# Gate and up tiles of two blocks at once, in seven products over gate/up, feature halves and blocks

## The chip, the cores and the metric

The kernel runs on one core of a Trainium2 chip. The metric is the device time of one execution in microseconds; the median of three runs is given. Five engines work side by side, each in the order of its own queue: TensorE (PE in the profile, its weight loads are PEld), VectorE (DVE), ScalarE (ACT), GpSimd (POOL) and SyncE (SP), which here issues every DMA.

## The reference, cut to what matters

A transformer block in fp32 on 2048 tokens with D = 576 features: attention with 32 query heads and one shared key and value head, then a bilinear feed-forward part with F = 4608 hidden features, both behind a layer norm and with a residual.

```python
h  = x + attention(layernorm(x)) @ wo
g  = layernorm(h) @ w_gate            # (2048, 576) @ (576, 4608)
u  = layernorm(h) @ w_up              # the same shape
h2 = h + (g * u) @ w_down             # (2048, 4608) @ (4608, 576)
```

## The kernel before, in words

Every fp32 product is made of three passes on rounded parts (type fp32r): each operand is split into a high part (a cast) and a low part (the operand minus its high part), and high x high, high x low and low x high are added in PSUM. `split` does it: the cast on the engine in `self.cast` (in the feed-forward part ScalarE, `act.copy`) or on one that is passed in, the subtraction on VectorE.

The tokens go in four blocks of 512 (`TB`), the hidden features in 36 tiles of 128 (`NF`), two tiles making a pair. `keys_values` and the loop behind it in `run` make keys, values and all queries, with the first block's attention between them: one round of that loop makes two attention steps (`pair`) and takes as much from `queries` as `RATE` allows. Then `blocks` runs `ffn(b)` for b = 0 to 3. The order of all engines' instructions is the order in which this Python code issues them (a manual schedule); there is no planner.

- `ffn(b)` makes, for each tile, `gate` and `up` by 27 matmuls each (9 groups of 64 features x 3 passes) on 64 rows of the array: gate on rows 0 to 63, up on rows 64 to 127, so that the two of a pair run side by side. `split_w` takes the weights (`wr`) apart, the cast on GpSimd, one tile ahead; `load_w` loads the next. Then `g` is copied from PSUM by ScalarE, and VectorE multiplies it with `up` into `hf`.
- The attention of blocks 1 to 3 runs between these matmuls while there is some left (`on`), two blocks ahead; it ends in tile 5 of block 2. From there to the end the tiles are made without it, with gate and up in one two-bank PSUM tile `gu`, of which there are two.
- `left_first`, `left` and `left_sums` prepare a pair of `hf` tiles for the down projection, which uses seven products instead of eight on a 2 x 2 split (a Strassen-Winograd scheme): four sums `S`, and the splits into `self.A`.
- `down(b, pair)` makes the down projection of a pair: 14 stages (`STAGES`) of three matmuls with full 128 rows and 288 columns, in three PSUM banks; 8 of the stages are added to the residual `h` by VectorE, 6 are copied to `tmp` by ScalarE and added by GpSimd. The weights `wdo` (seven tiles of 288 KB a pair) were split in block 0, stored to `wd_dram`, and are loaded by `load_wd` into ten buffers. The last pair of a block has 48 matmuls and no sums.
- `spread(b + 1)` transposes the next block's normed tokens into `X` and copies each half of the rows to the other by DMA, so that both row halves have them.
- `aux` is a queue of small things (normalising heads, output projections `project`, layer norm statistics and `scales`), taken in `run_aux` once or twice a tile.

Of the kernel before, what the change touches and what calls it, by code (L numbers as in the profile page):

```python
# [54 lines left out]
class Block:  # L55


    def __init__(self, tc, x, wq, wkv, wo, wo0, wgu, wd, cst, out):
# [3 lines left out]
        self.wgu, self.wd, self.cst, self.out = wgu, wd, cst, out  # L62
        self.pe, self.act, self.dve, self.sp = tc.nc.tensor, tc.nc.scalar, tc.nc.vector, tc.nc.sync
# [678 lines left out]
    def project(self, b, c):  # L742
# [27 lines left out]
        if c == 4:  # L770
            if b == 0:
                self.statistics(b, NQ - 1)
                self.normed[b] = self.mv, self.rstd(self.mv[:, :, 1], f"b{b}")
            else:
                last = b == NB - 1
                for i in range(4):
                    self.aux.append((self.round + i // 2, lambda i=i: self.some_statistics(b, i), self.within if last else None))
                if last:
                    self.aux.append((self.round + 2, lambda: self.scales(b), self.within))

# [6 lines left out]
    def some_statistics(self, b, s):  # L787

        self.statistics(b, s)
        if s == NQ - 1 and b < NB - 1:  # L790
            self.scales(b)
# [63 lines left out]
    def load_w(self, n):  # L855

        if n < NF * NB:
            r = self.wr[n] = self.wp.tile([P, 9, P], F32, tag="wr", bufs=1, name=f"wr{n}")
            self.sp.dma_start(r, self.wgu[n % NF])

    def split_w(self, n):
        if n < NF * NB:
# [37 lines left out]

    def down(self, b, pair):

        pe, dve, act, sp, pool = self.pe, self.dve, self.act, self.sp, self.nc.gpsimd
        h = self.h[b]
        W = [self.wdo.pop((b, pair, j), None) for j in range(7)]
        if pair == NC - 1:
            ys = {}

            def part(s, n, i):

                ms = [(self.A[:, k, 2 * i + s // 2], W[(1, 0, 2, 3)[2 * i + n]][:, l]) for k, l in ((0, 0), (0, 1), (1, 0))]
                for j, (m, k) in enumerate(ms):
                    pe.matmul(ys[s, n][:, :HD], m[:, s % 2 * P:(s % 2 + 1) * P], k, start=(i == j == 0), stop=(i == 1 and j == 2))  # L913
# [37 lines left out]
        for i, (t, bank, (x, w), first, (s, n), on_dve) in enumerate(STAGES):  # L951
            y = banks[bank]
            ms = [(self.A[:, k, x], W[w][:, l]) for k, l in ((0, 0), (0, 1), (1, 0))]
            for j, (m, k) in enumerate(ms):
                pe.matmul(y[:, :HD], m[:, t * P:(t + 1) * P], k, start=(first and j == 0), stop=(j == 2), skip_group_check=True)  # L955
            hs = h[:, t + 2 * s, n * HD:(n + 1) * HD]
            if on_dve:
                dve.tensor_tensor(hs, hs, y[:, :HD], ALU.add)  # L958
# [16 lines left out]
    def ffn(self, b):  # L975
        pe, act, dve = self.pe, self.act, self.dve
        X, hid, todo = self.X, [], None
        for f in range(NF):
            n_ = NF * b + f
# [10 lines left out]
            for c in range(9):  # L990
                for wk, xk in ((0, 0), (0, 1), (1, 0)):
# [52 lines left out]
            if f < NF - 1 and (on or not todo):  # L1044
                self.run_aux()
            todo = (f // 2,) if k else None
        if b + 1 < NB:
            both(self.spread(b + 1), self.down(b, *todo))
# [3 lines left out]
        else:  # L1052
            drain(self.down(b, *todo))

# [44 lines left out]
    def right(self, p):  # L1099
# [20 lines left out]
        self.load_raw(p + 1)  # L1120

    def begin(self, first):

        self.first = first
        self.wd_list = [(b, p, j) for b in range(first, NB) for p in range(NC) for j in (range(4) if p == NC - 1 else ORDER)]
        self.n_wd = 0
# [4 lines left out]
    def blocks(self):  # L1131
# [34 lines left out]
        self.load_x(2)  # L1166
        for b in range(NB):
            self.ffn(b)
        del self.A, self.o_hl, self.S, self.tmp, self.X, self.ob, self.mv

    def run(self):
# [3 lines left out]
        self.wd_dram = tc.dram_tile([NC, P, 7, 2, HD], F32, name="wd_dram")  # L1175
        self.m_dram = tc.dram_tile([NB, 2, H, TB], F32, name="m_dram")
        self.known, self.n_mx = [0] * NB, 0
        self.tqs, self.acc_at = [], 0
        self.begin(True)
        with ExitStack() as st:  # L1180
# [11 lines left out]
            with tc.tile_pool(name="p0q", bufs=1) as self.p0q:  # L1192
# [4 lines left out]
                with tc.tile_pool(name="qb", bufs=2) as self.qb:  # L1197
# [5 lines left out]
                    self.cast = self.dve.tensor_copy  # L1203
                    live, due = True, 0.0
                    while live:
                        if self.n_pair >= WO_FROM and not self.wo_r0:
                            for c in range(EARLY):
                                self.load_wo_0(c)
# [7 lines left out]
                        self.run_aux(1)  # L1216
                        self.flush(len(self.pend) - 1)
            self.wp, self.hh, self.late, self.hp2 = pool("w", 2), pool("hid", 4), pool("P3", LATE), pool("resid2", 1)
            self.blocks()
# [43 lines left out]
def f32(ap):  # L1263
    return ap.bitcast(F32)
# [100 lines left out]
```

## Time and profile before

| | |
|---|---|
| median of three runs | 2322.93 us (2322.11 to 2326.28) |
| the profiled execution | 2324.7 us, span of its instructions 2322.9 us |
| TensorE busy | 2285.7 us, 98% of the span |
| VectorE, ScalarE, GpSimd busy | 1202.2, 1410.1 and 684.9 us |
| first layer, keys and queries | to about 270 us |
| last attention step | 1674 us |
| block 2's tile 12 to the end | 1742 to 2322.9 us |

Busy times are unions over instructions; a matmul's end is modelled, so that neighbours overlap, and the time of one is read from the distance of starts. "Idle before, releaser" says how long an engine stood still before an instruction and which instruction's end let it go.

### The profile page before, as it was taken

To read this page: it belongs to the slowest core of one execution; us is meant where nothing else is said; L and a number is where in the kernel's file an instruction comes from. 1 tells how busy PE (TensorE), PEld (TensorE's weight loads), DVE (VectorE), ACT (ScalarE), POOL (GpSimd) and SP (SyncE) were. 2 spreads that over 40 slices of the span, in tenths; PEclk is the share of its full clock that TensorE was granted. 3 is DMA by queue.
4 is the path that set the end of the run, shared out by engine and by line. 5 is a ranking of instruction groups with operands and counts; after the bars stand their busy time and mean duration, and the time that the engine had idled before them with its cause. 6 is when DMAs were issued, how large, how long until landed. Compare 5 with 4: busy or idle time off the path is not lost.

```text
span 2322.9 us, 45901 instructions
## 1 busy us (share of the span) xinstructions
PE 2285.7 (98%) x18114; PEld 1589.5 (68%) x18114; DVE 1202.2 (52%) x2152; ACT 1410.1 (61%) x1877; POOL 684.9 (29%) x856
## 2 busy tenths in 40 slices
PE   7999999999999999999999999999999999999998
PEld 5333345676667666667766667766788888888887
DVE  8333435565565575434434444434476666466665
ACT  5899887767676767676776677676623233232322
POOL 4000003444354345212212212212233333333332
PEclk9999999999999999999999999999999999999999
DMA  5222305433442433543424333324354445554553
GB/s 172 80 77 70 99 30 154 148 108 122 141 149 94 140 132 113 182 138 113 122 84 129 113 95 119 126 88 151 106 184 169 169 169 183 195 169 169 175 180 123
DMA packets 127130, 306.76 MB, mean 132 GB/s; under 512 B 17553, under 2 KB 17681, under 8 KB 126265
## 3 DMA queue, kind: packets, MB, share of 16 engines
q1 hardware_dynamic: 126905, 303.73, 39.7%
q8 instruction: 145, 2.38, 0.4%
q14 instruction: 80, 0.66, 0.1%
HBM read 233.76 MB, written 55.67 MB: 125 GB/s over the span
## 4 chain that ended last, share of the span: by engine, by line
PE 79%; ACT 7%; DVE 6%; issue 4%; DMA 3%; SPq 1%; POOL 0%; ACTq 0%; DVEq 0%; POOLq 0%
PE acc L601 19%; PE y L955 16%; PE gu L997 13%; PE pg L997 12%; PE s L596 11%; ACT P L597 5%; PE yo L759 3%; PE pu L997 3%; PE psq L448 2%; DVE ws L89 1%; ACT room L88 1%; DVE hf L1031 1%; DVE S L892 1%; PE y L913 1%; DMA ob<-ob 1%
## 5 line engine op out<-in xcount | busy, mean ns | idle before, releaser
L597 ACT ACTIVATE P<-s 128x1024 f32<-128x1024 f32 x1024 | 1000.9, 1030 | 340.9 <-PE s L596 248.3
L997 PE MATMUL pu<-X,ws 64*128 64x512 f32 x2106 | 571.6, 390 | 0.4 <-DVE hf L1031 0.4
L997 PE MATMUL pg<-X,ws 64*128 64x512 f32 x2106 | 570.4, 389 | 0.0
L601 PE MATMUL acc<-P,V 128*32 128x512 f32 x4096 | 483.8, 597 | 0.0
L596 PE MATMUL s<-q,kT 56*128 56x512 f32 x2048 | 428.3, 426 | 11.5 <-ACT P L597 9.5
L997 PEld LDWEIGHTS pg<-X,ws 64*128 64x128 f32 x2106 | 389.9, 185 | 69.0 <-issue 1.2
L955 PE MATMUL y<-wdo,room 128*128 128x288 f32 x2856 | 414.9, 301 | 4.9 <-DVE h L958 4.4
L997 PE MATMUL gu<-X,ws 64*128 64x512 f32 x3564 | 417.0, 390 | 1.8 <-POOL ws L88 1.0
L955 PEld LDWEIGHTS y<-wdo,room 128*128 128x128 f32 x2856 | 386.9, 188 | 41.1 <-issue 23.6
L997 PEld LDWEIGHTS pu<-X,ws 64*128 64x128 f32 x2106 | 389.1, 185 | 5.6 <-DVE hf L1031 0.8
L997 PEld LDWEIGHTS gu<-X,ws 64*128 64x128 f32 x3564 | 341.9, 185 | 68.7 <-issue 6.2
L596 PEld LDWEIGHTS s<-q,kT 56*128 56x128 f32 x2048 | 192.0, 184 | 229.6 <-ACT P L597 132.4
L963 POOL TENSOR_TENSOR x<-x,tmp 128x288 f32<-128x288 f32 x204 | 157.6, 806 | 495.1 <-ACT tmp L962 494.8
L962 ACT COPY tmp<-y 128x288 f32<-128x288 f32 x408 | 163.0, 401 | 225.6 <-PE y L955 201.9
L88 POOL CAST ws<-wr 128x1152 fp32r<-128x1152 f32 x144 | 170.9, 1187 | 376.7 <-DMA wr<-in_wgu_dram 211.0
L601 PEld LDWEIGHTS acc<-P,V 128*32 128x32 f32 x4096 | 111.1, 109 | 249.0 <-issue 245.9
L89 DVE TENSOR_TENSOR ws<-wr,ws 128x1152 fp32r<-128x1152 f32 x144 | 201.4, 1399 | 96.1 <-POOL ws L88 94.7
L963 POOL TENSOR_TENSOR h<-h,tmp 128x288 f32<-128x288 f32 x204 | 158.9, 809 | 237.2 <-ACT tmp L962 237.0
L958 DVE TENSOR_TENSOR x<-x,y 128x288 f32<-128x288 f32 x272 | 117.8, 454 | 205.4 <-PE y L955 205.4
L1031 DVE TENSOR_TENSOR hf<-pu,g 128x512 f32<-128x512 f32 x78 | 54.0, 692 | 273.6 <-ACT g L1027 273.6
L958 DVE TENSOR_TENSOR h<-h,y 128x288 f32<-128x288 f32 x272 | 117.2, 453 | 83.9 <-PE y L955 83.6
L1027 ACT COPY g<-gu 128x512 f32<-128x512 f32 x66 | 38.9, 589 | 161.7 <-PE gu L997 161.7
(172 smaller groups left out, 1713.9 us busy)
## 6 DMA issues: line engine op xcount, KB each, us to landing
wdo<-wd_dram SPq DMA_DIRECT2D x369, 288.0 KB
wr<-in_wgu_dram SPq DMA_DIRECT2D x144, 576.0 KB
wd_dram<-wdo SPq DMA_DIRECT2D x123, 288.0 KB
q<-q_dram SPq DMA_DIRECT2D x64, 216.0 KB
raw<-in_wd_dram SPq DMA_DIRECT2D x36, 288.0 KB
q_dram<-qs SPq DMA_DIRECT2D x15, 504.0 KB
X<-X SPq DMA_DIRECT2D x24, 256.0 KB
ob<-ob SPq DMA_DIRECT2D x121, 36.0 KB
```

The source lines that it names most:

```text
L88: (copy or self.cast)(hi, src)
L89: self.dve.tensor_tensor(lo, src, f32(hi), ALU.subtract)
L596: self.pe.matmul(s_[:, i], self.kT[o:o + 56, t * P:(t + 1) * P], q[o:o + 56, pr], start=True, stop=True)
L597: self.act.activation(p_, s_, AF.Exp, scale=SCALE)
L601: self.pe.matmul(acc[32 * j:32 * j + 32, :], self.V[:, t, :], Ps[j // 2][:, j % 2, :], start=(t == 0), stop=(t == NT - 1), skip_group_chec ...
L759: pe.matmul(y[:, :HD], m, k, start=(i == 0), stop=(i == len(ms) - 1))
L955: pe.matmul(y[:, :HD], m[:, t * P:(t + 1) * P], k, start=(first and j == 0), stop=(j == 2), skip_group_check=True)
L958: dve.tensor_tensor(hs, hs, y[:, :HD], ALU.add)
L962: act.copy(z, y[:, :HD])
L963: pool.tensor_tensor(hs, hs, z, ALU.add)
L997: pe.matmul(ps, w[o:o + 64, wk, c], X[o:o + 64, xk, c], start=(j == 0), stop=(j == 26))
L1031: dve.tensor_tensor(hf, pu, g, ALU.mult)
```

## The change

Blocks 0 and 1, and the first `F1 = 12` tiles of block 2, stay as they are. What was left of the feed-forward part is done by a new function, `two_blocks`:

- the first 12 tiles of block 3 alone, in four products a tile: gate and up, each over two halves of the features. A half is 288 features: two groups of 128 rows, each in three passes, and a tail of 32 features whose three passes lie in 96 rows of one matmul. So a product has seven matmuls, all with more than 64 rows.
- the other 24 tiles for blocks 2 and 3 together. The 2 x 2 split is now over gate/up, feature halves and blocks, and seven products (with sums of weights on one side and differences of tokens on the other) take the place of eight.

The sums of the weights are made once, by `sums`, in the rounds of the projection loop, on GpSimd and VectorE, one step in each round, and are kept in DRAM (`s_dram`, and `t_dram` for the split tails). In `two_blocks` each product's weights are loaded (`load_raw_operand`), cast by ScalarE and completed by VectorE (`ahead`), five (alone: four) products ahead, with tails eight (six) ahead. Block 3's tokens are transposed in `transposed`, called step by step from `prepare` in block 2's tiles; the differences of tokens are made by `differences`, one step after each product of block 3's own tiles. `down` takes its left operand as an argument, and in the joint stage blocks 2 and 3 use the same loaded `wdo`. In the diff's core, `tt` and `add` are VectorE's `tensor_tensor`.

```diff
@@ project
-                             lambda: b in self.h and (c in self.wos and not (self.odd and (b == NB - 1 or b == 1 and c < 3)) if b else c in self.wo_in)))
+                             lambda: b in self.h and (c in self.wos and not (self.odd and self.more(NB) and (b == NB - 1 or b == 1 and c < 3)) if b else c in self.wo_in)))
                 for i in range(4):
-                    self.aux.append((self.round + i // 2, lambda i=i: self.some_statistics(b, i), self.within if last else None))
+                    self.aux.append((self.round + i // 2, lambda i=i: self.some_statistics(b, i), None))
@@ down
+        A = A or (self.A[:, 0], self.A[:, 1])
+        both = b == 2 and pair >= F1 // 2
         W = [self.wdo.pop((b, pair, j), None) for j in range(7)]
+        if both:
+            self.wdo.update(((b + 1, pair, j), w) for j, w in enumerate(W))
@@ ffn
-        for f in range(NF):
+        for f in range(F1 if b == 2 else NF):
...
+                    if n_ == N_OLD - 1 and j in (5, 20):
+                        self.first_operands(j > 5)
...
-                self.run_aux()
+                self.run_aux(1 + (b == 2))
+                self.prepare()
...
-            drain(self.down(b, *todo))
+            self.two_blocks(todo[0])
+    def tail(self, t, r):
+        self.act.copy(t, r)
+        self.dve.tensor_tensor(t[32:64], r[32:64], f32(t[32:64]), ALU.subtract)
...
+    def load_raw_operand(self, n):
+        if n < len(SEQ):
+            f, o = SEQ[n]
+            src = self.wj[f, o] if o < 4 else self.s_dram[f - F1, :, o - 4]
+            self.sp.dma_start(self.raws[n % 8], src.rearrange("p (c m) -> p c m", c=2))
+
+    def ahead(self, tails, splits):
+        while self.n_tail < min(tails, len(SEQ)):
+            f, o = SEQ[self.n_tail]
+            self.sp.dma_start(f32(self.slot(self.n_tail)[0:96, 4]), self.t_dram[f // 9, :, f % 9, o])
+            self.n_tail += 1
+        while self.n_split < min(splits, len(SEQ)):
+            w = self.slot(self.n_split)
+            self.split(w[:, 0:2], w[:, 2:4], self.raws[self.n_split % 8])
+            self.load_raw_operand(self.n_split + 8)
+            self.n_split += 1
+
+    def product(self, bank, n, B, first):
+        w, (hi, lo, t) = self.slot(n), B
+        ms = [(w[:, i + 2 * k], (hi, lo)[l][:, i]) for i in range(2) for k, l in ((0, 0), (0, 1), (1, 0))] + [(w[0:96, 4], t)]
+        for j, (a, m) in enumerate(ms):
+            self.pe.matmul(bank, a, m, start=(first and j == 0), stop=(j == 6), skip_group_check=True)
+        joint = n >= 4 * F1
+        self.ahead(n + 1 + (8 if joint else 6), n + 1 + (5 if joint else 4))
+
+    def left_parts(self, last, hf, A):
...
+        self.split(A[0][:, 0], A[1][:, 0], a11)
+        dve.tensor_tensor(S[:, 0], a21, a22, ALU.add)
+        dve.tensor_tensor(S[:, 1], S[:, 0], a11, ALU.subtract)
+        yield
+        dve.tensor_tensor(S[:, 2], a11, a21, ALU.subtract)
+        dve.tensor_tensor(S[:, 3], a12, S[:, 1], ALU.subtract)
+        yield
+        self.split(A[0][:, 3:7], A[1][:, 3:7], S)
+        yield
+        self.split(A[0][:, 1:3], A[1][:, 1:3], two(hf[1]))
+        yield
+
+    def two_blocks(self, pair):
...
+        queue = [(2, pair, (x() for x in [self.left_sums]))]
+        work = self.differences()
...
+        for f in range(F1):
+            head = queue.pop(0) if queue else None
+            for i, (bank, B) in enumerate(((x, 0), (x, 1), (y, 0), (y, 1))):
+                self.product(bank, n, self.B[B], i % 2 == 0)
...
+                if head:
+                    next(head[2], None)
+                if i == 1:
+                    act.copy(g, x)
+                if f:
+                    next(work, None)
+            dve.tensor_tensor(hf, y, g, ALU.mult)
...
+            if f % 2:
+                queue.append((3, f // 2, self.left_parts(False, hid, A)))
+            finish(head)
...
+        for f in range(F1, NF):
+            head = queue.pop(0) if queue else None
+            plan = [(x, 0, True), (y, 1, True), (x, "T2", False), (z, "T3", True), (x, "T1", False), (z, "T4", False), (x, "B22", False)]
+            for i, (bank, B, first) in enumerate(plan):
+                self.product(bank, n, self.B[B], first)
+                n += 1
+                if i == 0:
+                    act.copy(p1, x)
+                elif i == 1:
+                    add(p1, p1, y)
+                elif i == 2:
+                    act.copy(u2, x)
+                elif i == 3:
+                    act.copy(p7, z)
+                elif i == 4:
+                    add(p7, p7, x)
+                elif i == 5:
+                    add(u2, u2, z)
+                    dve.tensor_tensor(h3, p1, u2, ALU.mult)
+                if head:
+                    next(head[2], None)
+            dve.tensor_tensor(h2, p7, x, ALU.mult)
...
+            finish(head[:3] if head else None)
...
+        for b, p, parts, to in queue:
+            drain(self.down(b, p, to))
@@ sums
+    def sums(self):
...
+        def four(a, s):
...
+        for f in range(F1, NF):
+            a, s = f32(v[:, f % 2, 0]), f32(v[:, f % 2, 1])
+            four([a[:, o] for o in range(4)], [s[:, o] for o in range(4)])
+            yield
+            sp.dma_start(self.s_dram[f - F1], s)
+            load(f + 2)
+            yield
+F1 = 12
+N_OLD = 2 * NF + F1
+SEQ = [(f, o) for f in range(F1) for o in range(4)] + [(f, o) for f in range(F1, NF) for o in (0, 1, 5, 6, 4, 3, 7)]
```

`differences` has 28 steps: twelve subtractions or additions and four casts of 1024 columns, then six DMAs, and tails of 96 rows. `transposed` has three: the normed tokens (ScalarE, with copies of the tails on GpSimd); 16 transposes and their splits; eight transposes of tails and their parts. `finish` drains a queued pair's parts, issues its `down` and then the next `wdo` loads; after each second joint tile the pair is queued for block 2 and for block 3, to be taken one in each of the next two tiles. `four` makes four sums or differences of 256 columns on GpSimd. `sums` has 89 steps; those ahead of the ones shown make the sums of the tails, split them, and store 14 MB in `t_dram`.

More of the change, by code (lines that the diff above doesn't have):

```diff
@@ L789, in some_statistics @@
         self.statistics(b, s)
-        if s == NQ - 1 and b < NB - 1:
+        if s == NQ - 1:
             self.scales(b)
@@ new lines, in slot, with first_operands @@
+    def slot(self, n):
+        first = 4 * F1
+        return self.slots[n % 6 if n < first else (n - first) % 8]
+    def first_operands(self, split):
+        if not split:
+            self.slots = []
+            self.more_slots()
+            self.raws = [r[:, i] for t in ("wr", "wos") for r in [self.wp.tile([P, 4, 2, P], F32, tag=t, bufs=1, name=f"{t}_j")] for i in range(4)]
+            self.n_tail = self.n_split = 0
+            for n in range(8):
+                self.load_raw_operand(n)
+            self.ahead(3, 0)
+        else:
+            self.ahead(3, 3)
@@ new lines, in more_slots @@
+    def more_slots(self):
+        w = self.wp.tile([P, 3, 5, P], F32R, tag="ws", bufs=2, name=f"ws_j{len(self.slots)}")
+        self.slots += [w[:, i] for i in range(3)]
+    def load_raw_operand(self, n):
[13 more added lines that the diff above has]
+            self.n_split += 1
@@ new lines, in product @@
+    def product(self, bank, n, B, first):
[6 more added lines that the diff above has]
+    def left_parts(self, last, hf, A):
+        dve, S = self.dve, self.S
+        two = lambda x: x.rearrange("p (a q) -> p a q", a=2)
+        if last:
+            for i in range(2):
+                self.split(A[0][:, 2 * i:2 * i + 2], A[1][:, 2 * i:2 * i + 2], two(hf[i]))
+                yield
+            return
+        (a11, a21), (a12, a22) = (halves(x, HT) for x in hf)
+        self.split(A[0][:, 0], A[1][:, 0], a11)
+        dve.tensor_tensor(S[:, 0], a21, a22, ALU.add)
+        dve.tensor_tensor(S[:, 1], S[:, 0], a11, ALU.subtract)
+        yield
+        dve.tensor_tensor(S[:, 2], a11, a21, ALU.subtract)
+        dve.tensor_tensor(S[:, 3], a12, S[:, 1], ALU.subtract)
+        yield
+        self.split(A[0][:, 3:7], A[1][:, 3:7], S)
+        yield
+        self.split(A[0][:, 1:3], A[1][:, 1:3], two(hf[1]))
+        yield
@@ L1166, in blocks @@
         self.load_x(2)
-        for b in range(NB):
+        for b in range(NB - 1):
             self.ffn(b)
         del self.A, self.o_hl, self.S, self.tmp, self.X, self.ob, self.mv
+        del self.B, self.slots, self.raw, self.raw_tails, self.spare, self.prep
     def run(self):
@@ L1204, in run @@
                     live, due = True, 0.0
+                    sums = self.sums()
                     while live:
+                        next(sums, None)
                         if self.n_pair >= WO_FROM and not self.wo_r0:
@@ L1217, in run @@
                         self.flush(len(self.pend) - 1)
+                    drain(sums)
             self.wp, self.hh, self.late, self.hp2 = pool("w", 2), pool("hid", 4), pool("P3", LATE), pool("resid2", 1)
```

194 lines of the change are left out of this document (180 added, 14 removed).

## The prediction

> **What bounds the kernel now.** I read the page first (busy times, the chain that ended last), then a table of stretches, then the timeline of one cycle late in block 3. In order: the page's busy line and chain; the stretches (columns: stretch, its length, busy us of PE, PEld, DVE, ACT and POOL with instruction counts, granted clock, DMA share, GB/s); pieces of the chain.
>
> ```profile
> PE 2285.7 (98%) x18114; PEld 1589.5 (68%) x18114; DVE 1202.2 (52%) x2152; ACT 1410.1 (61%) x1877; POOL 684.9 (29%) x856
> PE 79%; ACT 7%; DVE 6%; issue 4%; DMA 3%; SPq 1%; POOL 0%; ACTq 0%; DVEq 0%; POOLq 0%
> ...
> 15.50:20.00 4.50, 3.82 (x16) 2.63 (x17) 4.37 (x9) 1.54 (x4) 4.15 (x4) 1.00 0.84 350
> 66.00:270.00 204.00, 204.00 (x1495) 77.23 (x1495) 60.96 (x110) 184.33 (x191) 0.00 (x0) 1.00 0.22 70
> 1742.40:2322.90 580.50, 568.17 (x4576) 489.40 (x4572) 350.64 (x592) 171.88 (x336) 207.43 (x241) 0.99 0.50 170
> ...
> 2060.31 6.36 PE gu L997 x53
> 2302.92 6.37 PE gu L997 x54
> ```
>
> From 1742 us on (block 2's tile 12 to the end) attention is over, and 568 of 580 us are matmul: only fewer or denser matmuls help there. The two chain pieces stand 13 cycles apart; a cycle is two feature tiles and one `down`, (2302.92 - 2060.31)/13 = 18.66 us. VectorE is 60% busy there, so it has room, but not twice over.
>
> The last 33 matmuls of one `down`, and a whole later cycle, in the timeline (start, us, engine, line, operation, count), in pieces cut small where single matmuls matter, with the durations that I use below:
>
> ```profile
> 1955.19 4.70 PE L955 MATMUL y<-wdo,room 128*128 128x288 f32 x33 [0.16 <-DVE h L958]
> ...
> 2053.54 0.61 PE L997 MATMUL gu<-X,ws 64*128 64x512 f32 x4
> 2054.09 0.53 PE L955 MATMUL y<-wdo,room 128*128 128x288 f32 x2
> 2059.94 0.86 DVE L958 TENSOR_TENSOR h<-h,y 128x288 f32<-128x288 f32 x2 [0.36 <-PE y L955]
> 2059.74 0.57 PE L955 MATMUL y<-wdo,room 128*128 128x288 f32 x3
> 2060.24 0.50 PE L997 MATMUL gu<-X,ws 64*128 64x512 f32 x2
> ...
> 2060.24 12.54 PE L997 MATMUL gu<-X,ws 64*128 64x512 f32 x108
> 2061.44 0.41 ACT L88 CAST room<-hf 128x256 fp32r<-128x256 f32 x1 [0.95 <-DVE hf L1031]
> 2063.59 0.42 DVE L89 TENSOR_TENSOR room<-hf,room 128x256 fp32r<-128x256 f32 x1
> 2066.75 0.59 ACT L1027 COPY g<-gu 128x512 f32<-128x512 f32 x1 [4.90 <-PE gu L997]
> 2067.37 0.69 DVE L1031 TENSOR_TENSOR hf<-gu,g 128x512 f32<-128x512 f32 x1 [3.36 <-ACT g L1027]
> 2067.63 1.15 POOL L88 CAST ws<-wr 128x1152 fp32r<-128x1152 f32 x1 [5.35 <-DMA wr<-in_wgu_dram]
> 2068.09 0.62 ACT L88 CAST room<-hf 128x512 fp32r<-128x512 f32 x1 [0.76 <-DVE hf L1031]
> 2068.09 0.96 DVE L892 TENSOR_TENSOR S<-hf,hf 128x256 f32<-128x256 f32 x1
> 2069.43 0.42 DVE L894 TENSOR_TENSOR S<-hf 128x256 f32<-128x256 f32 x1
> 2070.10 0.69 DVE L89 TENSOR_TENSOR room<-hf,room 128x512 fp32r<-128x512 f32 x1
> 2070.22 1.05 ACT L88 CAST room<-S 128x1024 fp32r<-128x1024 f32 x1 [1.51 <-DVE S L895]
> 2071.30 1.23 DVE L89 TENSOR_TENSOR room<-S,room 128x1024 fp32r<-128x1024 f32 x1 [0.51 <-ACT room L88]
> ```
>
> 54 pairs in 12.54 us, the last taking 0.39: (12.54 - 0.39)/53 = 0.229 a pair, 0.232 with the first pair's delay spread in. A matmul of `down` is (4.70 - 0.30)/32 = 0.1375, so 42 are 5.8 us.
>
> **The change, part by part.**
>
> *Fewer matmuls.* Now a tile of one block is 27 pairs of 64-row matmuls (gate beside up). After it, a tile of block 3 alone is 4 products of 7 matmuls = 28, and a tile of both blocks together 7 x 7 = 49 instead of 54. Over the range: 24 x 54 + 12 x 27 = 1620 slots become 24 x 49 + 12 x 28 = 1512, 108 fewer. What does a 128-row, 512-column matmul take? The key and query projections at the start are such:
>
> ```profile
> 34.36 3.41 PE L236 MATMUL psk<-XT,wk 128*108 128x512 f32 x14
> 1710.49 0.58 PE L955 MATMUL y<-wdo,room 128*128 128x288 f32 x3
> 1710.90 0.30 PE L759 MATMUL yo<-wos,room 128*128 128x288 f32 x1
> 274.02 1.35 PE L479 MATMUL psg<-tq,G 126*32 126x512 f32 x5
> L479 PE MATMUL psg<-tq,G x21: 388/397/426, 26.1 to 275.0; 126*32 126x512 f32 x17, 72*32 72x512 f32 x4
> ```
>
> (3.41 - 0.39)/13 = 0.232, the same as a pair. So 108 x 0.232 = **-25.1 us**.
>
> *No change of row grouping.* Today every `down` (128 rows) stands between tiles of 64 rows. The last pair before it ends at 2053.54 + 0.61 = 2054.15, so it began at 2053.76, and the first matmul of `down` begins at 2054.09: 0.33 us later where 0.23 is usual, some 0.09 lost. The first two matmuls of `down` end 0.53 after their start, so the second began 0.23 after the first where 0.1375 is usual: another 0.10. Going back, the last matmul of `down` begins at 2059.74 + 0.57 - 0.30 = 2060.01 and the next pair at 2060.24, 0.09 late, and that pair takes 0.50 instead of 0.39. So about 0.19 us each way. From `down` to the output projection, 128 rows after 128, the step is 1710.90 - (1710.49 + 0.28) = 0.13: nothing lost. In the range there are some 60 such changes (29 of `L955` and one of `L913` both ways), and in the new code everything has full rows: 60 x 0.19 = **-11.4 us**. Against it: the seventh matmul of each product has 96 rows, and if that were a grouping of its own, 216 products with two changes each would cost 216 x 2 x 0.19 = +82 us. But of the five `psg` matmuls above four have 126 rows and one 72, and all go in 1.35 us, (1.35 - 0.40)/4 = 0.24 each. I take nothing for it. The Trainium skill ("TensorEngine Tiling (Array Packing)", Key Properties) says that changing the tiling mode drains TensorE; the trace agrees, with 0.19 us each. Its list of configurations has 128, 64 and 32 rows, so by it too the tail is no mode of its own; taken as a drain at every change of a tile's shape it would speak against this change, with those 82 us.
>
> *Joint tiles: what VectorE and ScalarE must do.* Casts of weights go from POOL (one of 1152 columns) to ScalarE, seven of 256 columns a tile (0.41 each), with seven VectorE subtractions (0.42); three PSUM copies on ScalarE (0.59); three adds and two products of 512 on VectorE (0.69). Each tile also has a full left preparation (four sums of 0.42, splits of 256, 1024 and 512) and a `down` (8 adds). VectorE: 7 x 0.42 + 5 x 0.69 + 4 x 0.42 + 0.42 + 1.23 + 0.69 + 8 x 0.45 = 14.0 us of a tile's 49 x 0.232 + 5.8 = 17.2 us: 82%, and 10.4 of the 11.4 us of the products alone. There is one bank each for x, y and z, and x is read and rewritten within the tile, so the order counts. I follow one tile (product i ends at 1.62 x (i+1); an eviction starts 0.24 after the product, as `g` at 2066.75 after 27 pairs from 2060.24; both engines take their queue in order):
> - ScalarE: x copied 1.86 to 2.45, then the cast of a11 to 2.86. VectorE stands behind that cast: split to 3.31, two sums to 4.1, a weight split, the add of y to 5.05, two sums to 5.73.
> - ScalarE casts S 5.8 to 6.8, then a weight cast, the copy of z to 7.8 (the sixth product needs it at 8.12: just in time) and the 512 cast to 8.43. VectorE: split of S to 8.07, weight split, split of 512 to 9.15, weight split, the add of x into p7 to 10.10.
> - The seventh product rewrites x: it could start at 9.74 and starts at 10.2. Stall 0.46 us. After it VectorE is done with h2 at 12.75 and has both first adds of `down` done by 13.5; the fourth stage waits about as long as today (0.16 at 1955.19).
>
> 22 tiles have this load: 22 x 0.46 = **+10.1 us**. The bounds are 0 and 2.6 us a tile: one sum at 0.96 instead of 0.42, as at 2068.09 beside the POOL cast of 2067.63, moves the chain by 0.54, and there are four (0.46 + 4 x 0.54). I take 0.46, since the casts leave POOL. Tile 13 has no `down` after its products; there the next tile's first product waits for h2: **+1.2 us** (0.24 + 0.69 and a split).
>
> *Block 3's first 12 tiles.* Products 6.5 us a tile. In even tiles VectorE has 4 splits (1.7), the left preparation (4.0) and the last product (0.69); the differences for the joint stage add up to three operations of 1024 columns (1.2 each) in tiles 1 to 4, and tails in tile 6. So in tiles 2, 4 and 6 VectorE has some 9.5 us (neighbours overlap a little) for 6.5 us and its first add of `down` comes 2.5 us late: 3 x 2.3 = **+7 us** (0 to 10). Odd tiles have 5.8 in 6.5 us. Without these operations the same `down` would wait as today.
>
> Rows for the next three parts (two of TensorE's waits after 1980 us: total, times, longest; two of the timeline; one line's durations in ns, minimum, median, maximum):
>
> ```profile
> PE gu L997 <- POOL ws L88: 1.0, 1, 1.0
> PE gu L997 <- DVE ws L89: 0.7, 1, 0.7
> 2309.19 3.00 PE L913 MATMUL ye<-wdo,room 128*128 128x288 f32 x20
> 2312.39 3.97 PE L913 MATMUL ye<-wdo,room 128*128 128x288 f32 x28 [0.20 <-DVE room L89]
> L1088 POOL TENSOR_TENSOR sums<-raw,sums x17: 794/809/1811, 372.4 to 908.0; 128x288 f32<-128x288 f32 x17
> ```
>
> *Start.* The aux queue has block 3's last projection in tile 8 and statistics in 9, so the transposes come in tile 10 and the tails' in tile 11; the tail's cast stands behind `g`, the 512 cast and the copy on ScalarE: 0.24 + 0.59 + 0.69 + 0.62 + 2 x 0.59 + 0.69 = 4.0 us against 1.1 us of transposes and six matmuls: **+1.7**. The old change of block (transposes, shifted copies of X by DMA) goes; its waits, 1.7 us, go too, and four more transposes are 0.5: **-1**.
>
> *End.* Today the first half of the last `down` covers its splits (0.20 us idle). After, they stand behind the evictions of the `down` before: **+1**.
>
> *Sums in the projection stage (66 to 270 us).* POOL is idle there and VectorE 61 of 204 us, ScalarE 184. Some 93 rounds of 2.2 us take the 89 steps. Added: 96 POOL sums of 256 columns and the tails (about 95 us of POOL, at the 0.8 us for 288 columns above), and 40 MB of DMA, which with 70 GB/s of today makes 70 + 196 = 266 GB/s; 350 GB/s are seen at 15.5 us. A feature tile has two rounds (4.4 us) for 1 MB and 4 x 0.72 us of POOL, with two buffers: tight. SP issues in order, so a store that waits for POOL holds the loads of q (some 30 us ahead) and the head shuffles (12 steps, 13 us ahead). I take **+3 us**; from 0 (hidden) to 15 (the shuffles' lead used up).
>
> DMA after 1742 us is lighter: 7 x 176 KB and half of 2016 KB a joint tile are 2.2 MB in 17.7 us, 130 GB/s against 170 now; weights are loaded eight products ahead, at least one `down` and 11 us. SP's 17 issues a tile fit.
>
> Sum: -25.1 - 11.4 + 10.1 + 1.2 + 7 + 1.7 - 1 + 1 + 3 = **-13.5 us**. The profiled execution took 2324.7 us (span 2322.9), so 2311.2 of its kind; from the median of the runs, 2322.9 - 13.5 = **2309.4 us**.
>
> **Rivals.**
> - *All of it is covered.* VectorE's queue keeps up in the joint tiles and in tiles 2, 4 and 6, and the sums are hidden: the +10.1, +7 and +3 go, -33.6, **2289 us**. For it: VectorE idles 2 us at each tile's start in my chain, so a little more overlap pays at once. Against: every link of the chain has a row.
> - *The chain through x decides: slower.* ScalarE's cast of a11 behind the copy of x, VectorE's sums behind that, the add into p7 last. Each 0.1 us more on it costs 2.2 us. With two of the four sums at 0.96 the stall is 0.46 + 2 x 0.54, some 1.6 us a tile: 35.2 instead of 10.1: +11.6, **2334.5 us**. It decides from 0.46 + 13.5/22 = 1.07 us a tile. For it: the products need 10.4 of 11.4 us on an in-order engine; against: POOL, the cause of 0.96, has only its six adds, over about 1 us after `down`.
> - *The sums delay attention.* 15 us instead of 3: **2321 us**, no change. For: 266 of 350 GB/s; against: the leads named.
> - *Each 96-row tail changes the row grouping*: 2309.4 + 82 = **2391 us**; the `psg` row speaks against it. Weights that land late (their tails move in rows of 512 bytes, which no row here prices) would cost from nothing to the like.
>
> **How the numbers follow.** My case 0.45, all covered 0.17, the chain through x 0.22, attention delayed 0.10, the last 0.06. About 0.2% (4.6 us) is what can be told from no change. My case is faster nearly throughout (0.42, with 0.03 within); covered is faster; attention delayed is within 0.2%; of the two slow ones 0.02 come within. Faster 0.60, same 0.15, slower 0.25. My case alone is 2300 to 2318 us; for 8 in 10 the range takes in most of the covered case and of the chain through x: 2291 to 2336.
>
> **What would show it.** Right: `product`'s matmuls at 0.232 us, no late pair beside `down`; PE idle before the seventh product of each joint tile on VectorE's add into p7, some 0.5 us; in block 3's tiles 2, 4 and 6 `down` waiting 2 us for its first adds; 66 to 270 us not longer than 207. Wrong: PE waiting for ScalarE or DMA in the products, a longer projection stage, or full-row matmuls slower than 0.235.

## The result and the profile after

The changed kernel takes 2433.12 us (median of four runs, 2426.09 to 2435.74) against 2322.52 us for the kernel before on the same chip: a ratio of 1.0468, 95% interval 1.0443 to 1.0493. It is 4.7% slower, where 0.6% faster was forecast. The head of its page:

```profile
span 2433.8 us, 43851 instructions
PE 2298.8 (94%) x16390; PEld 1569.0 (64%) x16390; DVE 1270.2 (52%) x2410; ACT 1490.9 (61%) x2131; POOL 705.4 (29%) x921
```

TensorE was busy 98% of the span before and is busy 94% of a longer one: about 135 us of idle time (2433.8 - 2298.8) where there were 37. So waits were added, and the question is where. The two traces are cut at two places that both kernels have, the last attention step and the first matmul of the new stage (before: the tile at 1742.42 us that it replaces). The timelines of the changed kernel there (start, duration, engine, line, operation, and the idle time before it with its releaser; `L1215` is `product`):

```profile
1727.39 1.02 ACT L597 ACTIVATE P<-s 128x1024 f32<-128x1024 f32 x1 [1.79 <-PE acc L601]
...
1810.01 1.64 PE L1215 MATMUL js<-b,ws_j 128*128 128x512 f32 x6
```

| stretch | before | after | more | forecast |
|---|---|---|---|---|
| to the last attention step | 1676.2 | 1727.4 | +51.1 | +3 (sums) |
| from there to the new stage | 66.2 | 82.6 | +16.4 | nothing |
| the new stage, to the end | 580.5 | 623.8 | +43.3 | -16.5 (the other terms) |

The three add up to 110.8 us, and the runs differ by 110.6. (Step by step the first 51 us lie between attention steps 64 and 224: nothing until 64, 9.7 us at 80, 31.3 at 160, 49.4 at 224, and little after that. Those are the rounds that issue the sums.)

**The projection stage.** The windows view, 66 to 270 us (length, busy time of PE, PEld, DVE, ACT, POOL with instructions, clock, DMA share, GB/s); the same row of before stands in the prediction, with PE at 204.00 of 204:

```profile
66.00:270.00 204.00, 181.62 (x1265) 67.48 (x1267) 65.99 (x102) 155.86 (x161) 66.34 (x86) 0.93 0.71 217
```

TensorE stands 22 us and has done 1265 matmuls instead of 1495. No engine is full and the DMA engines are busy 0.71. What they wait for, in the view of waits from 66 to 270 us and, for SyncE's queue and the output projection, to 420 us (total, times, longest):

```profile
POOL sums L1402 <- DMA sums<-in_wjt_dram: 94.9, 4, 36.8
DVE sums L1414 <- POOL sums L1412: 50.4, 4, 17.8
DVE oT L88 <- DMA ob<-ob: 13.2, 1, 13.2
PE psq L448 <- DVE qs L455: 10.2, 2, 6.4
...
SPq L1433 <- POOL sums L1402: 64.3, 19, 7.0
SPq L1418 <- POOL sums L1412: 20.7, 4, 7.4
...
PE yo L759 <- POOL wo L88: 14.4, 1, 14.4
...
323.88 1.27 POOL L88 CAST wo<-wo_r 128x576 fp32r<-128x576 f32 x2 [11.68 <-DMA wo_r<-in_wo_dram]
```

`L1433` and `L1418` are the stores of the sums and of their tails. SyncE, which issues every DMA in order, stands 85 us before them until GpSimd is done; loads of queries, head moves and the next sums stand behind it. VectorE's subtraction (`L1414`) stands 50 us for GpSimd's cast, with the query evictions behind it. Two channels, then: the experiments have to tell which one counts.

The last two lines (the second from GpSimd's timeline) hold a third of the loss, the 16.4 us between attention steps 192 and 208. TensorE waits for the weights of the output projection (`wo`), whose cast on GpSimd waits 11.68 us for their load. SyncE issues the first of these loads at attention step 208 (318.56 us); in the kernel before it does so at step 202 (271.9 us). So this wait points at SyncE's queue as well.

**The joint tiles.** The waits of TensorE from 1725 us to the end:

```profile
PE js L1215 <- DVE raw L1288: 18.7, 24, 0.8
PE js L1215 <- ACT raw L1297: 16.2, 24, 0.7
PE js L1215 <- ACT g L1271: 8.3, 12, 0.7
PE y L956 <- ACT room L88: 5.1, 1, 5.1
...
PE js L1215 <- DVE hf L1275: 4.7, 6, 0.8
```

The counts speak: 24 joint tiles and 24 waits, twice; 12 own tiles and 12 waits. (`L1297` is the copy of x, `L1288` is `add`, `raw` the buffer that holds `p1`.) One tile's start:

```profile
2100.44 1.56 PE L1215 MATMUL js<-b,ws_j 128*128 128x512 f32 x6
2101.84 0.40 PE L1215 MATMUL js<-tails,ws_j 96*128 96x512 f32 x1
2102.91 1.67 PE L1215 MATMUL js<-b,ws_j 128*128 128x512 f32 x6 [0.67 <-ACT raw L1297]
2104.42 0.40 PE L1215 MATMUL js<-tails,ws_j 96*128 96x512 f32 x1
2105.60 0.50 PE L1215 MATMUL js<-X,ws_j 128*128 128x512 f32 x1 [0.78 <-DVE raw L1288]
```

The second product writes y and waits for ScalarE's copy of x; the third writes x and waits for VectorE's add of y. Neither touches the bank that it waits for. But x and y are the two banks of one PSUM tile, `js`. The evictions themselves are on time: the forecast's chain had the copy of x end 2.45 us into the tile and the add of y at 5.05, and the two products start at 2.47 and 5.16. With 2.47 and 2.69 us between starts instead of 1.63, a joint tile takes 19.5 us where the forecast had 17.7, and block 3's own odd tiles take 8.39 us where it had 6.5.

**Block 2's tiles 6 to 11.** The timeline of tile 10:

```profile
1786.77 3.14 ACT L1079 ACTIVATE xh<-h,mvb,yb 128x576 f32<-128x576 f32 x4 [6.06 <-DVE mvb L793]
1789.82 1.03 ACT L88 CAST room<-S 128x1024 fp32r<-128x1024 f32 x1
1790.90 0.85 PE L956 MATMUL y<-wdo,room 128*128 128x288 f32 x2 [5.14 <-ACT room L88]
```

ScalarE reaches the normalising of block 3's tokens 6.06 us before its statistics exist (`L793`), and the cast of `S` for the running `down` is behind it in its queue. Behind such a gap TensorE is also slower, as the windows view shows:

```profile
1790.00:1795.00 5.00, 2.15 (x6) 1.48 (x7) 3.73 (x4) 1.25 (x2) 2.33 (x4) 0.50 0.00 0
1795.00:1801.00 6.00, 6.00 (x33) 6.00 (x33) 1.98 (x5) 1.99 (x5) 3.14 (x5) 0.65 0.42 128
```

The granted clock is 0.50 and 0.65 there, and 18 matmuls of `down` follow each other at 0.24 us instead of 0.13.

### The profile page after: what moved, and what is told of

It reads as the page before. It is cut to its first block, busy times and chain, and to the rows that moved or that the text cites. A ratio compares the mean times of both kernels' runs of the same rounds, so it can differ in the third digit from the quotient of the medians.

```text
span 2433.8 us, 43851 instructions
## 1 busy us (share of the span) xinstructions
PE 2298.8 (94%) x16390; PEld 1569.0 (64%) x16390; DVE 1270.2 (52%) x2410; ACT 1490.9 (61%) x2131; POOL 705.4 (29%) x921
## 4 chain that ended last, share of the span: by engine, by line
PE 76%; ACT 6%; DMA 5%; DVE 5%; issue 4%; SPq 2%; POOL 1%; ACTq 0%; DVEq 0%; POOLq 0%
PE y L956 17%; PE acc L601 16%; PE js L1215 11%; PE pg L998 11%; PE s L596 9%; ACT P L597 5%; PE pu L998 3%; PE jz L1215 3%; PE yo L759 3%; DMA sums<-in_wj_dram 2%; PE gu L998 1%; POOL sums L1402 1%; SPq L1418 1%; DMA q_dram<-qs 1%; DMA t_dram<-sums 1%
## 5 line engine op out<-in xcount | busy, mean ns | idle before, releaser
L601 PE MATMUL acc<-P,V 128*32 128x512 f32 x4096 | 489.5, 603 | 12.0 <-DVE os L614 12.0
L956 PE MATMUL y<-wdo,room 128*128 128x288 f32 x2856 | 420.7, 304 | 11.0 <-ACT room L88 5.1
L956 PEld LDWEIGHTS y<-wdo,room 128*128 128x128 f32 x2856 | 395.1, 190 | 42.3 <-issue 13.4
L88 POOL CAST ws<-wr 128x1152 fp32r<-128x1152 f32 x84 | 100.9, 1202 | 201.1 <-PE pu L998 145.8
L1215 PE MATMUL js<-b,ws_j 128*128 128x512 f32 x504 | 134.6, 402 | 25.2 <-ACT raw L1297 12.1
L89 DVE TENSOR_TENSOR ws<-wr,ws 128x1152 fp32r<-128x1152 f32 x84 | 120.1, 1429 | 60.7 <-POOL ws L88 60.7
L89 DVE TENSOR_TENSOR room<-S,room 128x1024 fp32r<-128x1024 f32 x68 | 86.8, 1277 | 124.3 <-ACT room L88 124.1
L1402 POOL TENSOR_TENSOR sums<-sums 128x256 f32<-128x256 f32 (+1 forms) x116 | 84.4, 750 | 174.5 <-DMA sums<-in_wjt_dram 94.9
```

The costliest lines, as they stand in the source:

```text
L88: (copy or self.cast)(hi, src)
L89: self.dve.tensor_tensor(lo, src, f32(hi), ALU.subtract)
L601: self.pe.matmul(acc[32 * j:32 * j + 32, :], self.V[:, t, :], Ps[j // 2][:, j % 2, :], start=(t == 0), stop=(t == NT - 1), skip_group_chec ...
L1215: self.pe.matmul(bank, a, m, start=(first and j == 0), stop=(j == 6), skip_group_check=True)
L1402: pool.tensor_tensor(o, x, y, op)
```

## The experiments

Every ratio is to the kernel before, run on the same chip (medians of 2324.66 to 2327.35 us).

**y in the second tile.** Theory: a wait goes by the whole PSUM tile. Rival: VectorE and ScalarE are late by themselves.

```diff
-        hid, x, y, z = [], js[:, 0], js[:, 1], jz[:, 0]
+        hid, x, y, z = [], js[:, 0], jz[:, 1], jz[:, 0]
```

> In the changed kernel the second product of each joint tile starts 2.47 us after the first instead of 1.63, behind ScalarE's copy of x, though it writes y; the third starts 2.67 us later, behind VectorE's add that reads y, though it writes x. x and y are the two halves of one PSUM tile (js). Theory: the waits come from that sharing, not from a data dependence. Here y is the free half of z's tile (jz) and nothing else changes. Expected: both waits go (24 x 1.9 us), as do those of block 3's own tiles (12 x 0.8 and 6 x 0.9 us), 61 us; some 10 us may come back as the wait before the seventh product that the prediction named, which the slack hides now. 2375 us (2368 to 2388). Rival: ScalarE and VectorE are really late with the copy and the add, as the prediction's slow rival has it: the waits stay with y elsewhere, 2433 us.

Measured: 2380.21 us (ratio 1.022, 1.0203 to 1.0238). The same place of a joint tile:

```profile
2094.23 1.57 PE L1215 MATMUL js<-b,X 128*128 128x512 f32 x6
...
2095.88 1.55 PE L1215 MATMUL jz<-b,ws_j 128*128 128x512 f32 x6
...
2097.50 0.39 PE L1215 MATMUL js<-X,ws_j 128*128 128x512 f32 x1
```

No wait is left there, the starts are 1.65 and 1.62 us apart, the tile takes 17.6 us and the odd own tiles 6.51. The new stage takes 568.2 us (1811.26 to 2379.5): 55.6 less than in the changed kernel and 12.3 less than before. Here y shares a PSUM tile with z, and that still shows a little: the fourth product, which writes z, starts 4.97 us into the tile, right behind VectorE's add that reads y (it ends at 4.92), and its first two matmuls follow at 0.32 and 0.34 us instead of 0.23. TensorE, now earlier, waits more for VectorE's first adds of `down`:

```profile
PE y L956 <- DVE h L959: 11.3, 6, 3.7
```

**x and z in one tile.** The same theory the other way: the waits must go where the sharing goes.

```diff
-        hid, x, y, z = [], js[:, 0], js[:, 1], jz[:, 0]
+        hid, x, y, z = [], js[:, 0], jz[:, 0], js[:, 1]
```

> The doubled suspect: x and z share one PSUM tile (js) and y has a half of the other for itself. If sharing makes the waits, the second and third product start at once, but now the fourth (z behind the copy of x), the fifth (x behind the copy of z), the sixth (z behind the add that reads x) and the seventh (x behind the add that reads z) wait 0.85 to 1.05 us each: +3.7 - 1.9 = +1.8 us a joint tile, +43 us; block 3's own tiles have x and y apart and win some 15 us. 2461 us (2445 to 2475). If the engines are late of themselves: 2433 us, with the waits before the second and third product.

Measured: 2471.39 us (1.0624, 1.0606 to 1.0641), and the view of waits:

```profile
PE js L1215 <- DVE p L1288: 18.7, 24, 0.8
PE js L1215 <- DVE tail L1288: 18.7, 24, 0.8
PE js L1215 <- ACT p L1303: 16.3, 24, 0.7
PE js L1215 <- ACT tail L1301: 16.2, 24, 0.7
```

Four waits a tile instead of two, at the products that now share a tile: starts at 1.65, 1.62, 2.46, 2.58, 2.68 and 2.67 us. That engines are late by themselves falls: the same adds and copies hold nothing once the tiles are divided otherwise. The Trainium skill ("PSUM — Partial Sum Buffer", PSUM bank collisions raise a hardware error) advises to guard PSUM by bank and partition quadrant. The waits here span two banks, so they are wider than that rule asks for.

**No sums.** `sums = iter(())`; weights come from rows of other arrays of the same size, so the output is another one.

> Leaves out the sums of the weights altogether: the operands of the joint tiles are loaded from other arrays of the same shapes (so the result is another one), with as many bytes in as many rows of the same lengths. Attention's 1024 steps end 51 us later in the changed kernel than before; the loss comes in jumps up to step 208. Theory: all of it comes from the sums' work in the projection loop. Expected: the last attention step is back at 1676 us, the time 2382 us (2376 to 2388), and everything behind attention takes as long as in the changed kernel (706 us). Rival: part of the 51 us is a consequence of something else that the change moves (memory layout, the order of loads): more than 2390 us.

Measured: 2382.91 us (1.0246, 1.0229 to 1.0264); the last attention step is 1.4 us late instead of 51.1. The first stretch is the sums' alone.

**Subtraction on GpSimd.** Takes the wait off VectorE.

```diff
-            dve.tensor_tensor(r, f32(r), f32(hi), ALU.subtract)
+            pool.tensor_tensor(r, f32(r), f32(hi), ALU.subtract)
```

> The subtraction that makes the low parts of the sums of tails (five of 2048 columns) goes from VectorE to GpSimd. In the changed kernel VectorE stands 50 us in front of these five, in order, waiting for GpSimd, which waits for a load, which waits for the stores before it; behind them stand the evictions of the queries and of the attention sums. Theory A: VectorE's queue is the channel; 31 of the 51 us are lost in that part (steps 64 to 160), and most go: 2408 us (2400 to 2420). Theory B: SyncE's queue and the DMA traffic hold the loads and stores that attention needs itself; then at most a few us change: 2428 to 2440 us.

Measured: 2428.76 us (1.0441, 1.0424 to 1.0459), with the last attention step 44.9 us late. VectorE's queue is not the main channel; SyncE still stands as long:

```profile
SPq L1433 <- POOL sums L1402: 65.6, 19, 6.2
```

**Traffic alone.** All loads and stores of the sums, no arithmetic for them to wait for.

> Leaves out the sums' arithmetic (no GpSimd or VectorE work in the projection loop) and stores what lies in a buffer that is filled once, so that the same loads and stores are issued by SyncE at the same places without waiting for an engine. Theory B1 (SyncE's waits for engines): the loss goes nearly whole, 2388 us (2382 to 2400). Theory B2 (the bytes): it stays, 2415 to 2435 us.

Measured: 2383.19 us (1.0247, 1.023 to 1.0264), as without any sums:

```profile
66.00:270.00 204.00, 204.00 (x1495) 77.17 (x1495) 61.19 (x110) 184.33 (x191) 0.00 (x0) 1.00 0.85 274
```

274 GB/s at a DMA share of 0.85, and TensorE does not stand at all. Bytes and the number of issues cost nothing, nor do the 20.8 us (13 waits) that SyncE stands here for loads of the sums. This run leaves out the arithmetic with all its effects: SyncE's and VectorE's waits for it, and GpSimd's work beside VectorE's. The run before speaks against VectorE's waits; the ones below part the rest.

**Sums with a queue of their own.** Subtraction on GpSimd and `sp = self.nc.gpsimd` in `sums`: GpSimd computes and issues.

> With the subtraction on GpSimd the loss before attention's end stayed (+45 us at step 256), VectorE now standing for moved heads (ob, two waits of 13 us) and PE for a late weight of the output projection. Here, besides, all loads and stores of the sums are issued by GpSimd instead of SyncE; bytes and rows are the same. Theory B1: SyncE's order is the channel: it stands 65 us for GpSimd's sums and 20 for its casts, and the loads and moves that attention needs stand behind. Then most of the loss goes: 2395 us (2383 to 2408). Theory B2: the bytes themselves (40 MB more in about 230 us) fill the DMA engines and delay what attention needs whoever issues it: 2415 us or more.

Measured: 2463.87 us (1.0589, 1.0571 to 1.0606), slower than the change itself. The expectation missed, and the waits of TensorE from 66 to 420 us and GpSimd's timeline say why:

```profile
PE yo L759 <- POOL wo L88: 63.0, 1, 63.0
...
350.55 0.57 POOL L1433 DMA_DIRECT2D s_dram<-sums  x1 [0.30 <-POOL sums L1402]
353.79 1.27 POOL L88 CAST wo<-wo_r 128x576 fp32r<-128x576 f32 x2 [2.66 <-DMA s_dram<-sums]
```

The head moves and queries are freer of the sums now (12.3 us late at attention step 192, against 31.3 in the changed kernel). But GpSimd needs until 351 us for all of it, and the cast of the first output projection's weights (`wo`) stands behind the last sum in the same queue: one wait of 63 us. What made GpSimd so long, its groups from 70 to 350 us:

```profile
L1418 POOL DMA_DIRECT2D t_dram<-sums x58 | 28.3, 494 | 9.8 <-DMA t_dram<-sums 8.8 <-issue 0.6
L1424 POOL DMA_DIRECT2D sums<-in_wj_dram x24 | 18.8, 782 | 31.5 <-DMA sums<-in_wj_dram 19.2 <-issue 9.2 <-DMA t_dram<-sums 2.7
```

Issues of 0.5 and 0.8 us each, loads that it issues itself and then waits for, and 41.1 us (4 waits) until its own stores of tails have landed and their buffer can be loaded again. Without the one wait of 63 us the run would be at some 2463.9 - 63 = 2401 us, an estimate near the expectation. A run with that cast on another engine was not made.

**All but the sums mended.** y in the second tile; the transposed tokens taken later in block 2's tiles; the differences only in odd tiles, five steps in each instead of four in every tile; no sums.

```diff
+                    if j == 12 and n_ == N_OLD - 2:
+                        self.prepare()
...
-                if not on:
+                if not on and n_ != N_OLD - 3:
                     self.prepare()
...
-                if f:
+                if f % 2:
                     next(work, None)
+                    if i == 3:
+                        next(work, None)
```

> What the new scheme itself is worth: y apart from x, the sums left out (as in the run without sums, so another result), the normalising of block 3's tokens issued in the middle of tile 10 instead of at the end of tile 9 (ScalarE stood 6 us for the statistics there, with the split of S and so the down projection behind it), and the differences issued in block 3's odd tiles alone, which have no down projection behind them. Expected from the run with y apart: 2380 - 50 (sums) - 7 (normalising) - 11 (the waits of 2 to 5 us in block 3's tiles 2, 4 and 6) = 2312 us (2305 to 2322), that is 10 to 15 below before on the same chip. If the prediction's terms for matmuls and row grouping were wrong too, it is not below before.

Measured: 2316.8 us (0.9957, 0.994 to 0.9974). This is what the scheme could bring here with sums for nothing.

**The same with the sums on GpSimd alone.** These edits and the queue of their own.

> The same with the sums, made and moved by GpSimd alone: the candidate that computes the whole reference. If GpSimd's own queue is the cure it lies 0 to 12 us above the ceiling: 2318 us (2310 to 2326). If the bytes are the channel it lies 30 to 45 above it: 2350 us.

Measured: 2395.82 us (1.0292, 1.0275 to 1.0309), above both figures of the expectation. The same place decides (the longest of TensorE's waits from 70 to 420 us):

```profile
PE yo L759 <- POOL wo L88: 61.2, 1, 61.2
```

**Sums ordered ahead.** SyncE issues again, but a store should not be reached before its sum is done: it is issued three rounds after the sum instead of one, and loads run three features ahead in four buffers instead of two; tails go in single chunks with two buffers, their high part stored once. Core of the edit:

```diff
-        for f in range(F1, NF):
-            ...
-            sp.dma_start(self.s_dram[f - F1], s)
-            load(f + 2)
+        for f in range(F1, NF + 1):
+            if f < NF:
+                ...
+            if f > F1:
+                sp.dma_start(self.s_dram[f - 1 - F1], part(f - 1, 1))
+                load(f + 3)
```

Once with nothing else changed, once with the edits above.

> The changed kernel with this order of the sums alone. B1: last attention step back at 1676 to 1684 us, 2388 us (2383 to 2396). If waits move: 2400 us or more.

> The candidate for a version below both: y apart, normalising later, differences in odd tiles, and the sums kept on SyncE but issued so that SyncE does not meet a wait: every store two rounds behind its sum, every load three to six rounds ahead of its use (four buffers instead of two for the sums of the operands, the second pair in the tile of block 1's tokens, free by then; two small ones for the tails), the high part of the tails stored once and loaded twice. The traffic run says that bytes cost nothing, so theory B1 expects the run without sums plus at most 8 us: ratio to before 0.995 to 0.999. If the waits only move (the second DMA for each tail on SyncE, the chain load, sum, store still too long), it is above before, 1.005 to 1.02.

Measured: 2384.33 us (1.0255, 1.0239 to 1.027) for the first, and its row of the projection stage is that of before, with all sums made:

```profile
66.00:270.00 204.00, 203.79 (x1497) 76.97 (x1493) 84.04 (x120) 184.31 (x192) 102.04 (x141) 1.00 0.76 251
...
SPq L1446 <- POOL sums L1403: 12.8, 12, 2.5
DVE sums L1422 <- POOL sums L1418: 25.4, 5, 8.1
```

The second line, from the view of waits to 420 us, has SyncE's waits before the stores at 12.8 us instead of 64.3. GpSimd works 102.04 us in the stage instead of 66.34, beside VectorE, and nothing is lost by it. VectorE still stands 25.4 us for GpSimd's casts, at no cost. The loads of `wo` begin at attention step 202 again. So SyncE's queue, in its order and with the buffers that the order needs, was nearly all of the 51 us; the last attention step is 3.3 us late, and none of that by step 256. The Trainium skill ("DMA: Bandwidth & Descriptors", Anatomy of one DMA — SWDGE (gpsimd) path) says that any semaphore wait happens on the issuing sequencer, before the DMA is handed out. The trace agrees for SyncE, whose queue stood 64.3 us before the stores of the sums and 12.8 us with the new order.

With all edits: 2319.77 us (2317.4 to 2324.44, eleven runs; before 2324.66), ratio 0.9981 (0.9972 to 0.999). It is faster than the changed kernel and 0.2% below the kernel before, which is about what can be told from no change. Its last attention step starts at 1676.31 us, and the longest of TensorE's waits behind it are:

```profile
PE y L956 <- DVE h L959: 6.6, 6, 1.3
PE yo L759 <- DVE h L760: 2.6, 1, 2.6
PE js L1218 <- DVE tails L1105: 2.0, 1, 2.0
```

By stretch: +0.1, +13.4 and -18.4 us (562.0 instead of 580.5). The middle one eats most of the gain. Of it the output projection at tile 7's end takes 8.0 us instead of 3.3, `down` in tile 10 12.2 instead of about 6.5, and 24 transposes 2.7: 13.1 us. Only 5.8 us of the first two are waits that the view lists there (2.6, 1.9 and 1.3). Most of the rest is the slower clock behind them: 13 matmuls of the projection and 24 of `down` follow each other at 0.24 us instead of 0.13, some 4 us.

## Why the prediction was wrong

**Right.** *Full rows.* Matmuls of `product` follow each other at 0.23 us (2097.50 and the ones behind it), a product takes 1.63 us. *Row grouping.* In the last kernel:

```profile
1973.75 0.40 PE L1218 MATMUL js<-tails,ws_j 96*128 96x512 f32 x1
1973.99 6.18 PE L956 MATMUL y<-wdo,room 128*128 128x288 f32 x42
```

0.24 us into `down`, where 0.33 was seen at the change from 64 rows, and its second matmul follows at 0.14 where 0.23 was seen; a tail of 96 rows drains nothing. That rival falls, and so does late loading of weights: no product waits for a DMA. *The rest of the new stage.* The forecast's terms for it come to -16.5 us; with the banks apart it measured -12.3, and -18.4 with the differences moved too. Three small terms came near: in the last kernel the first tails are 2.0 us late (+1.7 forecast), the product behind tile 13 waits 0.8 us (+1.2), and the last `down` waits 1.2 us where 0.2 were (+1).

**Wrong, in order of size.** Two of the prediction's own signs of being wrong came, TensorE waiting for ScalarE in the products and a longer projection stage.

1. *"There is one bank each for x, y and z"*, in the joint tiles. True, but the chain followed there lets a product wait only for readers of its own bank, and that was false: the program's waits go by the PSUM tile. It cost two waits in each joint tile and one or two in each own tile, 55.6 us by the two traces. Nothing of it was in the sum or in a rival, and the profile of before did not raise the question, since its `gu` has two tiles that alternate.
2. *The sums: "I take +3 us; from 0 to 15".* The mechanism was named there (a store that waits for GpSimd holds the loads of q and the head shuffles), but sized by the leads of 12 steps and 30 us as if it came once. It came again and again, 23 waits of up to 7.4 us, and used the lead up: +51.1 us. The "attention delayed" rival had the right place at a third of the price. The counter-view, bandwidth, is refuted by 274 GB/s for nothing.
3. *Block 2's tiles 6 to 11* were costed at nothing beyond transposes: +16.4 us. Waits of 5.14, 2.6, 0.9 and 1.0 us and 2.7 us of transposes make 12.3 of it. Matmuls at the lower clock behind the waits make some 3 us more: 2 in `down`, and 1 in the tile behind the output projection, which takes 7.3 us instead of 6.4. The term looked at TensorE's work there, not at what stood in ScalarE's queue, nor at what a gap does to the clock.
4. *Differences:* +7 taken, with 2.3 us in each of tiles 2, 4 and 6. With the banks apart `down` waits there 2.35, 2.86 and 3.69 us, 8.9 in all: inside the range of 0 to 10, and 1.9 above what was taken.
5. *The chain through x: +10.1* was mis-sized the other way. In the last kernel the add into p7 ends 9.8 us after the tile's start (10.1 forecast) and the seventh product does not wait (its first weight load does, for 0.16 us, and hides it):

```profile
1970.74 0.40 PE L1218 MATMUL jz<-X,ws_j 128*128 128x512 f32 x1
1971.52 0.68 DVE L1293 TENSOR_TENSOR p<-p,js 128x512 f32<-128x512 f32 x1
1972.37 1.54 PE L1218 MATMUL js<-X,ws_j 128*128 128x512 f32 x6
```

The tile's 17.6 us agrees with the forecast's 17.7 all the same, by luck: the stall of 0.46 us is not there, but two starts are 1.71 and 1.73 us apart instead of 1.63, around the fourth product that waits for the add of y, and the last product and `down` take 7.64. Why these two take longer was not followed.

## What to carry to other kernels

Do not put an accumulation that is read into one PSUM tile with another that is written meanwhile: here two banks of one tile waited for each other's readers. On a queue that issues in order, place each store some rounds behind the engine that fills it, and look in the view of waits at the queue's own rows (SPq): 85 us of them used the lead up here, 12.8 did not. A bandwidth estimate says nothing about that. Before work is moved onto an idle engine, look for the small thing that stands next in its queue: here casts of 1.27 us cost 63.

## What was not expected of the hardware

- DMA at a share of 0.85 and 274 GB/s slowed neither TensorE nor attention: 2383.2 us with the traffic, 2382.9 without.
- A DMA that GpSimd issues takes 494 to 782 ns of GpSimd's own time (82 issues, 47 us, in the groups above), in the same queue as its arithmetic.
- The clock granted to TensorE falls with its gaps: 1.00 over 66 to 270 us in the kernels where it stands nowhere, 0.93 in the changed kernel (busy 181.62 of 204 us), and 0.78 over 270 to 420 us in the run with the sums' own queue (busy 85.43 of 150 us). A gap so costs more than its length: behind the one of 5.14 us, matmuls of `down` took 0.24 us instead of 0.13.
